# Late ZW rows in two column halves, the late rows of batches 4 to 7 behind later tiles, and three wide products beside the last weights

## The chip, the cores and the metric

The kernel runs on one core of a Trainium2 chip. TensorE (PE in the profile) multiplies matrices into PSUM banks of 128 partitions by 512 fp32 columns; PEld is its loading of stationary operands. VectorE is DVE, ScalarE is ACT, GpSimd is POOL, and SyncE (SP) only issues transfers here. The metric is the device time of one execution in microseconds, as the median of several runs.

## The reference

```python
# attention with a window of 128 and a bias that falls off with distance: 8 batches, 8 heads, 576 x 64
attn = softmax(where(mask, q @ k.T / 8 + bias, -1e9));  x = attn @ v      # heads joined: x is (8, 576, 512)
# mixing of modes
X  = rfft(x, axis=1)[:, :64]                   # 64 modes, complex
Yr = Xr @ w_r - Xi @ w_i;  Yi = Xr @ w_i + Xi @ w_r    # per mode a 512x512 matrix, two of them
y  = irfft(Y, n=576);  u = x + y
out = u + maximum(u @ w_ch, 0)
```

The two weight tensors w_r and w_i are 64 x 512 x 512 fp32 each, 134 MB in all; every byte is read once. The output is 9.44 MB of fp32.

## The kernel before

**Stages.** The attention runs over "units" (a pair of heads of one batch) while the first quarter of the weight rows streams in. Then the other three quarters of the weights stream in (from about 166 us on); TensorE multiplies each piece into an accumulator (`_modes`, L704) and between pieces prepares the end: `_xw` computes x + x @ w_ch per output tile and keeps it in two bf16 parts (`hl`), `_z_early` turns finished spectrum rows into Z (the spectrum itself) and ZW (the spectrum times w_ch) per batch.

**The tiles.** The output has 36 tiles of 128 rows by 512 columns (`g.seq`): four full tiles per batch, and after each odd batch one tile that holds the last 64 rows of two batches. Batch b of 0 to 7 comes in ascending order, so batches 4 to 7 begin at tile 18.

**The late rows.** The last modes are known only when the last weight piece has landed. Their spectrum rows (block 3 of `g.ZT`, 32 rows for each batch) are "late". `_modes` adds the last accumulator into ZT (DVE, L729). `_finish` then makes, for batches 0 to 3 and for batches 4 to 7, a late ZW (16 products of 128x512 in four column groups of TensorE, L790, tile `zlw`, cast to the bf16 tile `zl1`) and a late Z (16 products of 128x128, L794, tile `zlp`, cast to `zl0`). `_z_put` (POOL, L816) copies each batch's 32 late rows into the full Z or ZW tile.

**The end's loop.** For each tile, `g.u[i]` is a PSUM bank out of six. `_known(n)` starts it from `hl` (L745, a pair of products that share TensorE's columns); `_taken(n, 1)` adds the inverse transform of ZW (L825, a pair); `_greater(n)` takes the maximum with x on DVE (L845), which gives x + max(u @ w_ch, 0) and lacks only y; for the tiles in `RELU` it is a Relu on ACT (L843) and TensorE adds x by a further pair (L745). `_taken(i, 0)` adds y, the inverse transform of Z (a pair), ACT copies the bank to SBUF (L881, tile `o`, 16 buffers), and SP issues the transfer out (L886; the four tiles of two halves are two transfers, L889). The loop runs four tiles ahead (`AHEAD`): at tile i it starts tile i + 4. The first five tiles (`KNOWN`) are started before the last weights land and lack only their late rows; for them `_taken` uses the late tile directly. Each engine executes its instructions in the order in which the code emits them; there is no planner in this part.

In `_finish` the order was: late ZW of batches 0 to 3 (cast by ACT), late Z of 0 to 3 (cast by DVE), late ZW of 4 to 7 (cast by ACT), then the five known tiles' late products with the late Z of 4 to 7 after the second, then all 16 puts on POOL, then the loop.

**The last weight piece** arrives in three transfers (`LAST`: rows 0 to 2, 3 to 4, 5 of six), so the 24 products of the last `_modes` run as 12, 8 and 4, each group behind its own transfer.

Of the kernel before, what the change touches and what calls it, by code (L numbers as in the profile page):

```python
# [9 lines left out]
FP32 = mybir.dt.float32  # L10
BF16 = mybir.dt.bfloat16
# [5 lines left out]
P = 128  # L17
# [12 lines left out]
KNOWN = 5  # L30
# [2 lines left out]
FT_ROWS = (2, 3, 4, 5, 6)  # L33
FT_ORDERS = (10, 14, 18, 22)
WCH_ROWS = (1, 4)
RELU = (8, 16, 24, 32)
LAST = (0, 3, 5, 6)


# [5 lines left out]
def kernel(  # L45
# [52 lines left out]
    with tc.manual_schedule(engines={ET.SP, ET.PE, ET.Activation, ET.DVE, ET.Pool}):  # L98
        with ExitStack() as wctx:
# [129 lines left out]
            for m0, w in rest_w:  # L229
# [4 lines left out]
                if done in KNOWN_AT:  # L234
# [3 lines left out]
                    known = KNOWN_AT[done]  # L238
            mctx.close()
        _finish(g)  # L240


# [402 lines left out]
def _load_w(g):  # L645


    if g.loaded == len(g.parts):
        return False
    j, m0, w = g.parts[g.loaded]  # L650
    lo, hi = g.place[g.loaded]
    for u, z in g.place[g.used : g.loaded]:
        if u < hi and lo < z:
            return False
    g.loaded += 1
    r0 = GROUPS[j][0] * P
    src = (g.w_r, g.w_i)[w][m0 : m0 + JOINT[j], r0 : r0 + len(GROUPS[j]) * P]
    a = ROWS[j]
    cut = LAST if g.loaded == len(g.parts) else (0, a)
    for u, z in zip(cut, cut[1:]):  # L660
        g.nc.sync.dma_start(
            out=g.ring[:, lo + u * g.DM : lo + z * g.DM],
            in_=src.rearrange("m (p a) e -> p m (a e)", a=a)[:, :, u * g.DM : z * g.DM])
    return True
# [15 lines left out]
def _pair_of_modes(g, j, m0):  # L680
    for w in range(2):
        _modes(g, j, m0, w)
    if m0 % MB == MB // 2 - JOINT[j] and m0 + MB < g.NM:
        _select(g, j, m0 // MB * MB + MB)


def _modes(g, j, m0, w, last=False):


    nc = g.nc  # L690
    X = g.X[j, m0 // MB]
    assert g.parts[g.used] == (j, m0, w)
    lo, hi = g.place[g.used]
    wt = g.ring[:, lo:hi].bitcast(BF16)[:, 1::2].rearrange("p (a e) -> p a e", e=g.DM)
    ends = set(range(MB, g.NM + 1, MB)) | ({g.NM - 4, g.NM - 2} if last else set())
    if w == 0 and (m0 == 0 or m0 in ends):
        g.acc[j] = (m0, g.mpsum.tile([P, 4, 2, MB, 8], FP32, tag="acc", name="acc"))
    c0, acc = g.acc[j]
    R, n = ROWS[j], JOINT[j]
    order = [(et, a) for et in range(4) for a in range(R)]  # L700
    if g.used == len(g.parts) - 1:
        order = [(et, a) for u, z in zip(LAST, LAST[1:]) for et in range(4) for a in range(u, z)]
    for et, a in order:
        nc.tensor.matmul(  # L704
            acc[:, et, :, m0 - c0 : m0 - c0 + n, :],
            lhsT=wt[:, a, et * P : (et + 1) * P],
            rhs=X[:, a, 1 - w : 3 - w, m0 % MB : m0 % MB + n],
            start=(m0 == c0 and w == 0 and (et, a) == order[0]),
            stop=(m0 + n in ends and w == 1 and (et, a) == order[-1]))
    g.used += 1  # L710
    while _load_w(g):
        pass
    m = m0 + n - 1
    if w == 0 or m + 1 not in ends:
        return

    def rows(t):
        return t[:, c0 // 16, :, :, c0 % 16 : m % 16 + 1, :].rearrange("p e a m b -> p e a (m b)")

    acc = acc[:, :, :, 0 : m + 1 - c0].rearrange("p e a m b -> p e a (m b)")  # L720
    dst = rows(g.ZTa)
    if j == 0:
        nc.scalar.copy(dst, acc)
    else:
        o = dst
        if last:
            o = g.ZT[:, :, c0 // 16, :, c0 % 16 : m % 16 + 1, :].rearrange(
                "p e a m b -> p e a (m b)")
        nc.vector.tensor_tensor(out=o, in0=acc, in1=dst, op=ALU.add)  # L729


def _xt(g, n, pool, psum):
# [9 lines left out]
def _pair(nc, out, lhsT, rhs, **kw):  # L742

    for h in range(2):
        nc.tensor.matmul(  # L745
            out[64 * h : 64 * h + 64], lhsT=lhsT[h], rhs=rhs[h], tile_position=(0, 64 * h), **kw)


def _xw(g, n, xT, psum):
# [4 lines left out]
    xw = psum.tile([P, g.DM], FP32, tag="xw", bufs=2, name="xw")  # L754
    if n not in RELU:
        nc.tensor.matmul(xw, lhsT=g.ident_b, rhs=x, start=True, stop=False)
    for dt in range(4):
        nc.tensor.matmul(  # L758
            xw, lhsT=xT[:, dt], rhs=g.wch[:, dt],
            start=(dt == 0 and n in RELU), stop=(dt == 3))  # L760
    for h in range(2):
# [21 lines left out]
        nc.gpsimd.memset(g.ZW[b][32 * (b % 4) : 32 * (b % 4) + 32], 0.0)  # L783


def _z_product(g, ps, w, et, k, l):

    ks = slice(32 * k, 32 * k + 32)
    if w:
        g.nc.tensor.matmul(  # L790
            ps[ks], lhsT=l, rhs=g.wch[:, et], start=(et == 0), stop=(et == 3),
            tile_position=(0, 32 * k))
    else:
        g.nc.tensor.matmul(  # L794
            ps[ks, et], lhsT=l, rhs=g.ident_b, start=True, stop=True,
            tile_position=(0, 32 * k))


def _z_late(g, b0, w, pool, tag, copy):


    ps = g.eps.tile([P, 4, P], FP32, tag="zp", name="zlp") if w == 0 else (
        pool.tile([P, g.DM], FP32, tag=tag, name="zlw"))
    for et in range(4):
        for c in range(4):
            l = g.ZT[:, et, 3].rearrange("p a m b -> p (a m) b")[:, :, b0 + c]
            _z_product(g, ps, w, et, c, l)
    t = g.fin.tile([P, g.DM], BF16, tag=f"zl{w}", bufs=2, name=f"zl{w}")
    copy(t, ps if w else ps.rearrange("p a b -> p (a b)"))
    g.late[w, b0] = t  # L810


def _z_put(g, w, b):

    ks = slice(32 * (b % 4), 32 * (b % 4) + 32)
    g.nc.gpsimd.tensor_copy((g.Z, g.ZW)[w][b][ks], g.late[w, b // 4 * 4][ks])  # L816


def _taken(g, i, w, late=None):

    rows = slice(0, 32) if late else slice(0, P)
    for h, (b, s) in enumerate(g.seq[i][1]):
        o = slice(32 * (b % 4), 32 * (b % 4) + 32) if late else rows
        z = late if late else (g.Z, g.ZW)[w][b]
        g.nc.tensor.matmul(  # L825
            g.u[i][64 * h : 64 * h + 64], lhsT=g.FT[o, b % 4, s : s + 64], rhs=z[o],
            start=False, stop=(w == 0 or late is not None or i >= KNOWN),
            tile_position=(o.start, 64 * h), skip_group_check=(w == 0))


def _known(g, i):

    pool, tag = ((g.fps, "f0"), (g.fps, "f1"), (g.lps, "l0"), (g.lps, "l1"), (g.lps, "l2"),
                 (g.kps, "k0"))[i % 6]
    g.u[i] = pool.tile([P, g.DM], FP32, tag=tag, name="u")
    _pair(g.nc, g.u[i], [g.ident2] * 2, [g.hl[:, i, h] for h in range(2)],
          start=True, stop=False)


def _greater(g, i):  # L840

    if i in RELU:
        g.nc.scalar.activation(g.u[i], g.u[i], AF.Relu)  # L843
    else:
        g.nc.vector.tensor_tensor(out=g.u[i], in0=g.u[i], in1=g.seq[i][0], op=ALU.max)  # L845


def _finish(g):

    nc, tc = g.nc, g.tc
    N = len(g.seq)
    with ExitStack() as fctx:
        g.fin = pool = fctx.enter_context(tc.tile_pool(name="fin", bufs=16))
        g.kps = fctx.enter_context(
            tc.tile_pool(name="kps", bufs=1, space=bass.MemoryType.PSUM, side="right"))
        _z_late(g, 0, 1, g.eps, "zwp", nc.scalar.copy)
        _z_late(g, 0, 0, g.eps, "zp", nc.vector.tensor_copy)
        _z_late(g, 4, 1, g.kps, "k0", nc.scalar.copy)  # L860
        for i in range(KNOWN):
            _taken(g, i, 1, g.late[1, 0])
            _greater(g, i)
            if i == 1:
                _z_late(g, 4, 0, g.eps, "zp", nc.scalar.copy)
        for w, b in ((0, 0), (1, 1), (0, 1), (1, 0), (1, 2), (0, 2), (1, 3), (0, 3)):
            _z_put(g, w, b)
        for b in range(4, 8):
            for w in (1, 0):
                _z_put(g, w, b)  # L870
        for i in range(N):
            x, n = g.seq[i][0], i + AHEAD
            if i in RELU:
                _pair(nc, g.u[i], [g.ident_b[:, 0:64], g.ident_b[:, 64:128]], [x] * 2,
                      start=False, stop=True, skip_group_check=True)
            _taken(g, i, 0)
            if KNOWN <= n < N:
                _known(g, n)
                _taken(g, n, 1)
            o = pool.tile([P, g.DM], FP32, tag="o", name="o")  # L880
            nc.scalar.copy(o, g.u[i])  # L881
            if KNOWN <= n < N:
                _greater(g, n)
            _, (lo, hi) = g.seq[i]
            if hi == (lo[0], lo[1] + 64):
                nc.sync.dma_start(out=g.out[lo[0], lo[1] : lo[1] + P], in_=o)  # L886
            else:
                for h, (b, s) in enumerate((lo, hi)):
                    nc.sync.dma_start(out=g.out[b, s : s + 64], in_=o[64 * h : 64 * h + 64])  # L889
# [30 lines left out]
```

## Time and profile before

| what | value |
|---|---|
| runs before | 445.66, 448.30, 448.21 us; median 448.21 |
| the profiled execution | 450.29 us; the span of its instructions 448.5 us; mean granted clock 0.769 |
| busy | PE 294.1, PEld 204.2, DVE 216.1, ACT 189.6, POOL 139.1 us |
| DMA | 173.86 MB, mean 388 GB/s |
| stage from the last weight piece on (about 414 us) | 34 us |
| output transfers | 32 of 256 KB, 3.3 us median to landing; 8 of 128 KB, 3.1 us |

The page's second part cuts the span into 40 slices of 11.2 us; the digits give the busy tenths of each engine, the granted TensorE clock and the share of the DMA engines. Windows of the trace give the same for any stretch. The timeline gives groups of instructions in order of time, with the start, the duration, and in brackets the idle time of the engine before it and what ended that.

### The profile page before, as it was taken

What the parts mean: (1) busy time and instruction counts of PE and PEld (TensorE: products, weight loads), DVE (VectorE), ACT (ScalarE), POOL (GpSimd) and SP (SyncE); (2) the same over time, 40 slices, a digit from 0 to 9 for tenths busy, and PEclk for the clock granted to TensorE, in tenths of its full rate; (3) what the DMA queues carried; (4) which work ended last, traced back from release to release, by engine and by line L of the source; (5) the groups of instructions that cost most, each with busy time, mean ns of one, the idle gap of its engine ahead of it and who ended that gap; (6) DMA issues with size and microseconds to landing.
All of it is one profiled execution on the core that took longest, in us unless ns stands there. A gap on an engine that the chain in (4) does not pass through costs nothing.

```text
span 448.5 us, 12893 instructions
## 1 busy us (share of the span) xinstructions
PE 294.1 (66%) x5506; PEld 204.2 (46%) x5527; DVE 216.1 (48%) x427; ACT 189.6 (42%) x302; POOL 139.1 (31%) x257
## 2 busy tenths in 40 slices
PE   2467989887787885222235664854856748696993
PEld 2455767666666763111123333432433334464661
DVE  8458566566765661010002543453535345462882
ACT  3787656584866741000011331322313233251794
POOL 7699889586876702020000000000000000000700
PEclk9969576686988975555555988589778587899997
DMA  8999999999999999999999999999999999996498
GB/s 249 346 335 327 388 325 353 347 390 379 392 368 375 393 415 429 432 425 426 430 427 433 426 429 429 427 430 426 430 429 430 426 429 430 427 428 282 185 374 288
DMA packets 51562, 173.86 MB, mean 388 GB/s; under 512 B 4912, under 2 KB 21296, under 8 KB 43440
## 3 DMA queue, kind: packets, MB, share of 16 engines
q1 hardware_dynamic: 51120, 171.99, 97.2%
q0 software_dynamic: 384, 1.05, 0.9%
q8 instruction: 43, 0.70, 0.6%
q14 instruction: 15, 0.12, 0.1%
HBM read 163.58 MB, written 9.44 MB: 386 GB/s over the span
## 4 chain that ended last, share of the span: by engine, by line
DMA 50%; PE 26%; ACT 10%; DVE 6%; issue 4%; POOL 2%; ACTq 0%; POOLq 0%
DMA ring<-in_moe_w_r_dram 47%; ACT att L459 6%; PE acc L704 5%; PE sc L447 4%; PE xt L539 4%; PE u L825 3%; PE av L493 3%; DMA ring<-in_moe_w_i_dram 3%; ACT qkT L428 3%; PE tqk L420 2%; PE u L745 2%; POOL qkb L397 1%; PE xw L758 1%; DVE x_sb L507 1%; ACT mask L311 1%
## 5 line engine op out<-in xcount | busy, mean ns | idle before, releaser
L704 PE MATMUL acc<-Xz,ring 128*128 128x32 bf16 x2048 | 70.7, 183 | 100.2 <-DMA ring<-in_moe_w_r_dram 51.0
L704 PEld LDWEIGHTS <-ring 128*128 128x128 bf16 x2048 | 61.3, 101 | 130.1 <-DMA ring<-in_moe_w_r_dram 65.1
L763 ACT CAST hl<-xw 64x512 bf16<-64x512 f32 x72 | 41.7, 579 | 105.6 <-PE xw L758 70.9
L459 ACT ACTIVATE att<-sc 128x1024 bf16<-128x1024 f32 x64 | 65.6, 1025 | 32.8 <-PE sc L447 26.7
L764 DVE TENSOR_TENSOR hl<-xw,hl 64x512 bf16<-64x512 f32 x72 | 49.6, 688 | 58.1 <-ACT hl L763 57.8
L409 POOL CAST vb<-v 64x256 bf16<-64x256 f32 x128 | 64.7, 505 | 20.1 <-PE av L493 13.7
L783 POOL MEMSET ZTa<- 32x512 bf16 x2 | 1.0, 515 | 187.5 <-ACT ZTa L781 187.5
L447 PE MATMUL sc<-qkT,qkT 64*64 64x256 bf16 (+1 forms) x512 | 32.4, 330 | 30.1 <-ACT qkT L428 16.3
L758 PE MATMUL xw<-wch,xT 128*128 128x512 bf16 x138 | 46.3, 467 | 2.7 <-issue 2.2
L428 ACT COPY qkT<-tqk 128x576 bf16<-128x576 bf16 x64 | 40.7, 638 | 0.6 <-PE tqk L420 0.6
L420 PE MATMUL tqk<-ident_b,qkb 64*64 64x64 bf16 x1152 | 31.7, 214 | 7.6 <-POOL qkb L397 6.9
L420 PEld LDWEIGHTS <-qkb 64*64 64x64 bf16 x1152 | 30.8, 130 | 10.2 <-POOL qkb L397 9.2
L464 DVE TENSOR_TENSOR att<-att,mask 128x1024 bf16<-128x1024 bf16 x32 | 26.9, 839 | 14.7 <-ACT att L459 14.5
L585 ACT ACTIVATE Xz<-xz 128x192 bf16<-128x192 f32 (+1 forms) x24 | 7.5, 313 | 59.0 <-DVE Xz L584 57.9
L493 PE MATMUL av<-vb,att 128*128 128x65 bf16 (+1 forms) x512 | 30.8, 215 | 0.6 <-issue 0.2
L584 DVE CAST Xz<-xz 128x384 bf16<-128x384 f32 (+1 forms) x24 | 12.0, 511 | 36.4 <-PE xz L578 35.7
L447 PEld LDWEIGHTS <-qkT 64*64 64x64 bf16 x512 | 13.1, 120 | 35.3 <-ACT qkT L428 18.8
L397 POOL CAST qkb<-k 128x576 bf16<-128x576 f32 x32 | 27.5, 859 | 0.0
L493 PEld LDWEIGHTS <-att 128*128 128x128 bf16 (+1 forms) x512 | 24.4, 111 | 6.5 <-issue 0.6
L397 POOL CAST qkb<-q 128x576 bf16<-128x576 f32 x32 | 24.6, 768 | 6.1 <-PE tqk L420 3.3
L738 DVE COPY xT<-tp 128x512 bf16<-128x512 bf16 x36 | 15.2, 421 | 21.9 <-PE tp L736 21.4
L469 DVE TENSOR_TENSOR att<-att,mask 128x1024 bf16<-128x1024 bf16 x32 | 25.0, 780 | 1.5 <-ACT att L459 1.1
(104 smaller groups left out, 395.2 us busy)
## 6 DMA issues: line engine op xcount, KB each, us to landing
ring<-in_moe_w_r_dram SPq DMA_DIRECT2D x32, 1536.0 KB, 13.8
ring<-in_moe_w_i_dram SPq DMA_DIRECT2D x31, 1536.0 KB, 13.7
ring<-in_moe_w_i_dram SPq DMA_DIRECT2D x33, 512.0 KB, 8.0
ring<-in_moe_w_r_dram SPq DMA_DIRECT2D x32, 512.0 KB, 7.4
q<-in_q_dram SPq DMA_DIRECT2D x32, 288.0 KB, 6.3
k<-in_k_dram SPq DMA_DIRECT2D x32, 288.0 KB, 6.2
v<-in_v_dram SPq DMA_DIRECT2D x64, 128.0 KB, 5.8
out_dram<-o SPq DMA_DIRECT2D x32, 256.0 KB, 3.3
```

What stands on the lines that cost most here:

```text
L397: g.nc.gpsimd.tensor_copy(tb, t)
L409: g.nc.gpsimd.tensor_copy(o[64 * r : 64 * r + 64, i], v[64 * i : 64 * i + 64, r])
L420: g.nc.tensor.transpose(tp[hs, r, :], u.b[w][hs, r], g.ident_b[hs, hs], tile_position=(64 * hh, 64 * hh))
L428: g.nc.scalar.copy(dst.rearrange("c (p r) -> c p r", r=g.R), u.tp[w].rearrange("c r p -> c p r"))
L447: nc.tensor.matmul(sc[64 * r : 64 * r + 64, hh, 256 * i : 256 * i + nq], lhsT=kT[hs, c * P + r : c * P + P : 2], rhs=qT[hs, c * P : c * P ...
L459: nc.scalar.activation(a, sc, AF.Exp, scale=1.0 / math.sqrt(g.D))
L464: nc.vector.tensor_tensor(out=a, in0=a, in1=m, op=ALU.mult)
L493: nc.tensor.matmul(av[o, hh, col(t)], lhsT=att[c // 2][:, hh, q0 : q0 + m], rhs=u.vb[:, 2 * c + hh, 0 : D + 1], start=(j == 0), stop=(t < ...
L704: nc.tensor.matmul(acc[:, et, :, m0 - c0 : m0 - c0 + n, :], lhsT=wt[:, a, et * P : (et + 1) * P], rhs=X[:, a, 1 - w : 3 - w, m0 % MB : m0 ...
L758: nc.tensor.matmul(xw, lhsT=xT[:, dt], rhs=g.wch[:, dt], start=(dt == 0 and n in RELU), stop=(dt == 3))
L763: nc.scalar.copy(g.hl[own, n, h], xw[own])
L764: nc.vector.tensor_tensor(out=g.hl[other, n, h], in0=xw[own], in1=g.hl[own, n, h], op=ALU.subtract)
```

## The change

The diff touches `_finish` and what it calls, one set of tile numbers, and the last `_modes`.

- `RELU` becomes (8, 13, 15, 24, 32) in place of (8, 16, 24, 32): tiles 13 and 15 take the Relu on ACT and the added pair on TensorE, tile 16 takes the maximum on DVE. `_xw` accordingly leaves out the product with the identity for 13 and 15 and makes it for 16.
- Around the last weight piece, `_wide` makes one 128x512 product of the identity with w_ch into the bank `zp`, whose result is not used: before the second group, before the third, and after the last.
- The late ZW of batches 0 to 3 is made in two column halves, in the banks `zwp` and `k0`: 16 products of 256 columns, cast by ACT; 16 products of 256 columns, cast by DVE. The late Z of 0 to 3 is cast by ACT. For tile 0, the late product is made once per half.
- The late ZW of batches 4 to 7 moves into the loop: four of its 16 products behind each of tiles 3, 5, 7 and 9, the cast on DVE and one put on POOL behind tile 9. The late Z of 4 to 7 follows behind tile 11, with its cast on DVE and the other seven puts.

```diff
-RELU = (8, 16, 24, 32)
+RELU = (8, 13, 15, 24, 32)
+ZW_LATE = (3, 5, 7, 9)
+Z_LATE = 11
...
     for et, a in order:
+        if g.used == len(g.parts) - 1 and (et, a) in [(0, u) for u in LAST[1:-1]]:
+            _wide(g)
         nc.tensor.matmul(
...
+    if g.used == len(g.parts) - 1:
+        _wide(g)
     g.used += 1
...
+def _wide(g):
+
+    ps = g.eps.tile([P, 4, P], FP32, tag="zp", name="wide")
+    g.nc.tensor.matmul(
+        ps.rearrange("p a b -> p (a b)"), lhsT=g.ident_b, rhs=g.wch[:, 0], start=True, stop=True)
...
-        _z_late(g, 0, 1, g.eps, "zwp", nc.scalar.copy)
-        _z_late(g, 0, 0, g.eps, "zp", nc.vector.tensor_copy)
-        _z_late(g, 4, 1, g.kps, "k0", nc.scalar.copy)
+        sides = [slice(0, g.DM // 2), slice(g.DM // 2, g.DM)]
+        zl = _late(g, 0, 1)
+        for c, p, tag, copy in (
+                (sides[0], g.eps, "zwp", nc.scalar.copy),
+                (sides[1], g.kps, "k0", nc.vector.tensor_copy)):
+            ps = p.tile([P, g.DM], FP32, tag=tag, name="zlw")[:, c]
+            _z_late(g, 0, 1, range(4), ps, c)
+            copy(zl[:, c], ps)
+        zp = g.eps.tile([P, 4, P], FP32, tag="zp", name="zlp")
+        _z_late(g, 0, 0, range(4), zp)
+        nc.scalar.copy(_late(g, 0, 0), zp.rearrange("p a b -> p (a b)"))
         for i in range(KNOWN):
-            _taken(g, i, 1, g.late[1, 0])
+            for c in sides if i == 0 else [slice(0, g.DM)]:
+                _taken(g, i, 1, zl, c, last=(c.stop == g.DM))
             _greater(g, i)
-            if i == 1:
-                _z_late(g, 4, 0, g.eps, "zp", nc.scalar.copy)
...
-        for b in range(4, 8):
-            for w in (1, 0):
-                _z_put(g, w, b)
         for i in range(N):
...
+            if i in ZW_LATE:
+                if i == ZW_LATE[0]:
+                    zwp = g.eps.tile([P, g.DM], FP32, tag="zwp", name="zlw")
+                _z_late(g, 4, 1, [ZW_LATE.index(i)], zwp)
+            if i == ZW_LATE[-1]:
+                nc.vector.tensor_copy(_late(g, 4, 1), zwp)
+                _z_put(g, 1, 4)
+            if i == Z_LATE:
+                zp = g.eps.tile([P, 4, P], FP32, tag="zp", name="zlp")
+                _z_late(g, 4, 0, range(4), zp)
+                nc.vector.tensor_copy(_late(g, 4, 0), zp.rearrange("p a b -> p (a b)"))
+                for w, b in ((0, 4), (1, 5), (0, 5), (1, 6), (0, 6), (1, 7), (0, 7)):
+                    _z_put(g, w, b)
             o = pool.tile([P, g.DM], FP32, tag="o", name="o")
```

More of the change, by code (lines that the diff above doesn't have):

```diff
@@ L783, in _z_early, with _z_product @@
         nc.gpsimd.memset(g.ZW[b][32 * (b % 4) : 32 * (b % 4) + 32], 0.0)
-def _z_product(g, ps, w, et, k, l):
+def _z_product(g, ps, w, et, k, l, cols=slice(0, 512)):
     ks = slice(32 * k, 32 * k + 32)
@@ L790, in _z_product @@
         g.nc.tensor.matmul(
-            ps[ks], lhsT=l, rhs=g.wch[:, et], start=(et == 0), stop=(et == 3),
+            ps[ks], lhsT=l, rhs=g.wch[:, et, cols], start=(et == 0), stop=(et == 3),
             tile_position=(0, 32 * k))
@@ L796, in _z_product, with _z_late, _late @@
             tile_position=(0, 32 * k))
[L799 to L804, printed above, removed]
+def _z_late(g, b0, w, ets, ps, cols=slice(0, 512)):
+    for et in ets:
         for c in range(4):
             l = g.ZT[:, et, 3].rearrange("p a m b -> p (a m) b")[:, :, b0 + c]
[L807 to L810, printed above, removed]
+            _z_product(g, ps, w, et, c, l, cols)
+def _late(g, b0, w):
+    g.late[w, b0] = g.fin.tile([P, g.DM], BF16, tag=f"zl{w}", bufs=2, name=f"zl{w}")
+    return g.late[w, b0]
 def _z_put(g, w, b):
@@ L816, in _z_put, with _taken @@
     g.nc.gpsimd.tensor_copy((g.Z, g.ZW)[w][b][ks], g.late[w, b // 4 * 4][ks])
-def _taken(g, i, w, late=None):
+def _taken(g, i, w, late=None, cols=slice(0, 512), last=True):
     rows = slice(0, 32) if late else slice(0, P)
@@ L825, in _taken @@
         g.nc.tensor.matmul(
-            g.u[i][64 * h : 64 * h + 64], lhsT=g.FT[o, b % 4, s : s + 64], rhs=z[o],
-            start=False, stop=(w == 0 or late is not None or i >= KNOWN),
+            g.u[i][64 * h : 64 * h + 64, cols], lhsT=g.FT[o, b % 4, s : s + 64],
+            rhs=z[o, cols],
+            start=False, stop=last and (w == 0 or late is not None or i >= KNOWN),
             tile_position=(o.start, 64 * h), skip_group_check=(w == 0))
```

## The prediction

> **What bounds the kernel now.** I read the slices of the page first, then windows of the end, then its timeline, and last the landing times of the transfers out.
>
> ```profile
> PE   2467989887787885222235664854856748696993
> PEclk9969576686988975555555988589778587899997
> DMA  8999999999999999999999999999999999996498
> 412.38:415.79 3.41, 2.32 (x48) 1.46 (x47) 0.29 (x1) 0.00 (x0) 0.00 (x0) 1.00 0.12 48
> 415.79:419.20 3.41, 3.41 (x68) 1.73 (x62) 2.45 (x4) 2.01 (x4) 2.09 (x4) 1.00 0.01 2
> 429.44:439.68 10.24, 10.24 (x98) 6.73 (x96) 8.73 (x14) 9.53 (x18) 0.00 (x0) 1.00 1.01 370
> 439.68:443.10 3.42, 1.29 (x11) 0.50 (x6) 0.83 (x2) 2.29 (x5) 0.00 (x0) 1.00 1.00 359
> ```
>
> The DMA engines are full in nearly every slice; the hole is the 37th and 38th (403.6 to 426.1 us). The clock (tenths) changes while weights stream and is high in the last slices. Until about 412 us the weights set the time and nothing of the change lies on their path. In the windows (length; busy PE, PEld, DVE, ACT, POOL; clock; DMA share; GB/s) the DMA engines stand nearly still from 412.4 to 419.2 and are then full to the end. So the end has two parts: about 5 us from the last weights to the first transfer out, and some 27 us in which 9.44 MB go out. In the second part PE is busy without a gap as well.
>
> ```profile
> 414.51 0.29 DVE L729 TENSOR_TENSOR ZT<-acc,ZTa 128x128 bf16<-128x128 f32 x1 [5.90 <-PE acc L704]
> 414.86 1.09 PE L790 MATMUL zlw<-wch,ZT 128*32 128x512 bf16 x16 [0.38 <-DVE ZT L729]
> 416.00 0.58 ACT L809 CAST zl<-zlw 128x512 bf16<-128x512 f32 x1 [6.63 <-PE zlw L790]
> 416.01 1.05 PE L790 MATMUL zlw<-wch,ZT 128*32 128x512 bf16 x16
> 417.00 0.62 PE L825 MATMUL u<-zl,FT 32*64 32x512 bf16 x4
> 417.44 6.88 DVE L845 TENSOR_TENSOR u<-u,x_sb 128x512 f32<-128x512 f32 x11 [0.51 <-PE u L825]
> 417.54 0.47 PE L794 MATMUL zlp<-ident_b,ZT 128*32 128x128 bf16 x16
> 418.50 0.70 PE L825 MATMUL u<-ZTa,FT 128*64 128x512 bf16 x4
> 418.94 2.82 ACT L881 COPY o<-u 128x512 f32<-128x512 f32 x5 [0.29 <-PE u L825]
> 419.55 4.74 SPq L886 DMA_DIRECT2D out_dram<-o  x8
> 442.27 2.02 SPq L886 DMA_DIRECT2D out_dram<-o  x4
> ```
>
> This is the first part as a chain: ZT, late ZW, cast, tile 0's late product, its maximum, its last product, its copy, its transfer. Between 416.01 and 418.0 PE also does the late rows of batches 4 to 7, which no tile before 18 needs. The last line is the tail: the last four issues; the copy they wait for had ended at 442.27, the last issue began at 443.89 and landed at 447.30.
>
> **The first part, changed.** Late ZW: 16 products of 512 columns take 0.92 us (414.86 to the next group at 415.78). With 256 columns the streaming halves, but there are 16 weight loads in each half, and 16 such loads of the late Z take 0.41 (417.54 to 417.95) to 0.49 us. I take 0.49 a half (bounds 0.46, half of 0.92, and 0.66, PEld's own busy time for 16): the two halves end at 415.84 instead of 415.78, no gain by themselves. The gain is in what follows. The second half's cast on DVE starts at about 416.05 and costs 0.42 (128x256 from PSUM, L584, 421 ns) in place of ACT's 0.585; ACT's half (between 330 ns for 192 columns, L585, and 585 for 512; by a straight line 0.38) is over before. Late Z takes 0.41, to 416.25. Tile 0's second half goes at about 416.55 instead of 417.00, since the second late ZW (416.01 to 416.93) is no longer ahead of it. Its maximum runs from 416.9 to 417.6. The other four known tiles need 4 x 0.2155 = 0.86 (a pair every 0.2155 us, from 422.24, 422.46, 422.68, 422.89), to 417.5. Late Z of 0 to 3 is now cast by ACT behind its half: 416.5 to 417.1; the first put on POOL (0.60) ends at 417.75. So tile 0's last product goes at about 417.8 instead of 418.49: **0.7 us earlier**, and the first transfer at 418.9. Bounds: 0.35 if the halves are bound by loads at 0.66 each, 0.85 if they take 0.46 and ACT's cast is not late.
>
> **The loop, changed.** PE does 3 pairs a tile, 0.645 us, and never waits; what is added there comes out later, tile by tile. Late ZW of 4 to 7: four products behind each of four tiles, 0.92 / 4 = 0.23 each (bounds 0.2155, one stream of 512 columns, and 0.27), 0.92 in all. Late Z: 0.41 (0.23 to 0.47). RELU has one tile more: one pair, 0.2155. Sum 1.55 us (1.3 to 1.8). Against 0.7 gained at the start, PE is earlier by 0.7 up to tile 3, level at about tile 9, and **0.85 us later from tile 17 to the end**. DVE gains two casts of 0.69 and loses one maximum of 0.70, and at tiles 9 and 11 the casts stand where the maxima of 13 and 15 stood; behind them wait the maxima of 14 and 16, which PE needs 3 us later. ACT gains a Relu of 0.58 in the loop (ahead of it, its three casts become one and a half); it is busy 9.53 of 10.24, so two Relus within three tiles press it, for about 0.5 us, under a lead of four tiles. Puts: 0.61 each; the first of batch 4 ends near 426.6, tile 18's first use is at tile 14, near 428.7; the seven others run from 427.8 to 432, and the next user is tile 18 at 431.2, which needs only the first two. With late casts this cover of 2 us goes, and each us beyond is a stop of PE. SP's list is the same.
>
> **Wide products.** 0.2155 each, in PE's gaps of 0.45 (413.14 to 413.59, waiting for the second transfer), 0.25 (to 414.21) and 0.38 (to 414.86, waiting for DVE's ZT). They cost nothing there; if the three transfers land together, the first two cost 0.43. The loss of two identity products in `_xw` and the gain of one (0.2 us each) lie under PE's 51 us of waiting for weights.
>
> The row on the clock: the window 412.38 to 415.79 has PE at 68% and the clock stays at 1.00; windows of 3.41 us at 26 to 32% (340.70, 364.59) were each followed by 0.50. [...]
>
> **The transfers out.** A tile's 128 rows go at 0.636 us a tile (landings 437.12, 437.75, 438.38 ...), 22.9 us for 36. First bytes moved at 420.43, last near 446.6: 26.2 us, so 3.3 us were lost. Two losses stand out: blocks of code for PE (queue q8, 16 KB a packet) at 420.30 for 1.33 us and 434.62 for 0.94 us; around the second no tile landed between 434.68 and 437.12, 1.8 us more than the rhythm. [...] Both loads stay: the first shifts by about 24 PE instructions, to near 421.2, the second some 40 instructions earlier, to near 433.
>
> Sum: the stream can start at 419.7, 0.7 earlier, and would end 0.7 earlier if it never waited. But from tile 12 on PE's lead is gone: tile 18 is ready for the stream (issue plus 0.87 to the first byte) at about 433.5, when the stream is through tile 17 at 432.9; it waits 0.5. In the tail, PE's 0.85 is hidden: SP's last issues lag the copies by 1.6 us, and the last landing comes 3.41 us after its issue where 2.6 is the shortest. Result: -0.7 + 0.5 = **-0.2 us**. On the profiled execution 450.29 - 0.2 = 450.1; that execution is 2.1 over the median, and I take the difference onto the median: **448.0 us**.
>
> **Rivals.**
> - *The early start is passed on whole* (stream never waits, because the first code load leaves a queue of finished tiles): -0.7, 447.5. For it: transfers were full from 422.5. Against it: issues and copies kept step up to tile 18 (2.65 us to landing, the shortest).
> - *PE's debt decides, slower*: the loop becomes PE's from tile 9 on, copies and SP keep no lag, and the last landing follows PE's end by as much as before: +0.85, 449.1. It decides if the lag of 1.6 us at SP's tail was made of its own issue time (0.5 to 0.65 an issue) and is made again behind later copies. For it: SP's last seven issues are spaced by SP alone. Against it: that lag grew behind one issue of 1.14 us at 434.92, during the code load.
> [...]
> - *The change misses its aim*: halves bound by loads, start only 0.35 earlier, debt 1.2: about +0.3, 448.5.
>
> **How the numbers follow.** Forecast 0.42, passed on whole 0.18, PE's debt 0.18, clock 0.10, aim missed 0.12. Cases run from 446.5 to 449.1; the bounds of the unknown costs add 0.4 on either side, and the three runs of before lie 2.6 apart, so a median moves by about 1: 445.5 to 449.8. About 1% (4.5 us) is what a measurement of this kernel can tell from no change, and no case comes near it: faster 0.03, same 0.94, slower 0.03.
>
> **What would show it.** First transfer issued near 418.9 after ZT at the same time; four groups of 0.23 us of `zlw` in the loop; PE's last product near 441.7 instead of 440.9; DMA below full for half a us around 433. I am wrong if PE stops in the loop (puts or casts late), if the three weight transfers bunch, or if the clock falls to 0.50 in the end.

## The result

The changed kernel is **slower by 0.44%**: the ratio to the kernel before is 1.0044 with a 95% interval of 1.0024 to 1.0064; medians 449.83 us (22 runs, 447.31 to 453.66) against 448.03 us (22 runs, 445.52 to 451.23). On 448 us that is 2.0 us, with an interval of 1.1 to 2.9 (the medians alone differ by 1.8). The forecast was 0.2 us faster; the measured median lies 0.03 us above the upper end of the range, on the side of the rival "PE's debt decides".

### The profile page after: what moved, and what is told of

Same layout as the page of the kernel before. It is cut to its first block, busy times and chain, and to the rows that moved or that the text cites. A ratio compares the mean times of both kernels' runs of the same rounds, so it can differ in the third digit from the quotient of the medians.

```text
span 446.8 us, 12938 instructions
## 1 busy us (share of the span) xinstructions
PE 296.9 (66%) x5528; PEld 202.8 (45%) x5549; DVE 217.0 (49%) x428; ACT 190.2 (43%) x302; POOL 138.3 (31%) x257
## 3 DMA queue, kind: packets, MB, share of 16 engines
q0 software_dynamic: 384, 1.05, 1.0%
## 4 chain that ended last, share of the span: by engine, by line
DMA 60%; PE 23%; ACT 7%; DVE 4%; issue 3%; SPq 2%; POOL 1%; ACTq 0%; POOLq 0%
DMA ring<-in_moe_w_r_dram 46%; DMA ring<-in_moe_w_i_dram 7%; PE acc L708 4%; DMA v<-in_v_dram 4%; ACT att L461 4%; DMA k<-in_k_dram 3%; PE u L838 3%; PE xt L541 3%; PE sc L449 3%; PE av L495 2%; ACT qkT L430 2%; PE u L758 2%; PE tqk L422 2%; SPq L364 1%; PE xw L771 1%
## 5 line engine op out<-in xcount | busy, mean ns | idle before, releaser
L708 PE MATMUL acc<-Xz,ring 128*128 128x32 bf16 x2048 | 69.8, 183 | 99.5 <-DMA ring<-in_moe_w_i_dram 50.8
L708 PEld LDWEIGHTS <-ring 128*128 128x128 bf16 x2048 | 60.4, 101 | 129.6 <-DMA ring<-in_moe_w_i_dram 63.6
L411 POOL CAST vb<-v 64x256 bf16<-64x256 f32 x128 | 61.2, 478 | 23.1 <-PE av L495 16.2
L771 PE MATMUL xw<-wch,xT 128*128 128x512 bf16 x139 | 45.2, 456 | 2.6 <-issue 2.0
L422 PE MATMUL tqk<-ident_b,qkb 64*64 64x64 bf16 x1152 | 32.6, 217 | 9.1 <-POOL qkb L399 8.6
L495 PE MATMUL av<-vb,att 128*128 128x65 bf16 (+1 forms) x512 | 32.2, 220 | 0.5 <-DVE att L471 0.3
L495 PEld LDWEIGHTS <-att 128*128 128x128 bf16 (+1 forms) x512 | 25.6, 115 | 6.7 <-issue 0.9
L399 POOL CAST qkb<-q 128x576 bf16<-128x576 f32 x32 | 26.5, 829 | 4.4 <-PE tqk L422 1.6
```

The source lines that it names most:

```text
L399: g.nc.gpsimd.tensor_copy(tb, t)
L411: g.nc.gpsimd.tensor_copy(o[64 * r : 64 * r + 64, i], v[64 * i : 64 * i + 64, r])
L422: g.nc.tensor.transpose(tp[hs, r, :], u.b[w][hs, r], g.ident_b[hs, hs], tile_position=(64 * hh, 64 * hh))
L495: nc.tensor.matmul(av[o, hh, col(t)], lhsT=att[c // 2][:, hh, q0 : q0 + m], rhs=u.vb[:, 2 * c + hh, 0 : D + 1], start=(j == 0), stop=(t < ...
L708: nc.tensor.matmul(acc[:, et, :, m0 - c0 : m0 - c0 + n, :], lhsT=wt[:, a, et * P : (et + 1) * P], rhs=X[:, a, 1 - w : 3 - w, m0 % MB : m0 ...
L771: nc.tensor.matmul(xw, lhsT=xT[:, dt], rhs=g.wch[:, dt], start=(dt == 0 and n in RELU), stop=(dt == 3))
```

## The profile after

The span of the profiled execution is 446.8 us, shorter than the 448.5 us before, although the kernel is slower. The two executions differ in when the last weights arrive, which the change does not touch: DVE finished ZT at 414.81 us before and at 411.63 us after. So everything below is counted from the end of that ZT. The slices and, for the end, four windows of the changed kernel (columns as before: length; busy PE, PEld, DVE, ACT, POOL; clock; DMA share; GB/s):

```profile
PE   2578889887887885232236565665766549688993
PEclk9999856686698885555556996868879888899998
DMA  8999999999999999999999999999999999995598
411.34:415.46 4.12, 3.57 (x69) 2.16 (x69) 2.53 (x6) 1.57 (x4) 1.67 (x3) 1.00 0.01 2
415.46:429.44 13.98, 13.98 (x142) 6.76 (x140) 11.23 (x18) 11.24 (x20) 7.21 (x14) 1.00 0.79 290
429.44:439.68 10.24, 10.24 (x96) 5.45 (x92) 8.66 (x14) 9.27 (x19) 0.55 (x1) 1.00 0.97 347
439.68:443.10 3.42, 0.21 (x2) 0.00 (x0) 0.00 (x0) 1.51 (x4) 0.00 (x0) 0.99 0.99 345
```

The hole before the first transfer is 4.12 us from the start of ZT's addition, where it was 5.04 (414.51 to 419.55). But in the 14 us that follow, PE is busy without a gap and the DMA engines run at a share of 0.79, where it was 0.92 in the same 13.98 us behind the first issue before (419.55 to 433.53): they wait for tiles. The timeline of the changed kernel shows both:

```profile
411.34 0.29 DVE L735 TENSOR_TENSOR ZT<-acc,ZTa 128x128 bf16<-128x128 f32 x1 [6.21 <-PE acc L708]
411.68 1.10 PE L803 MATMUL zlw<-wch,ZT 128*32 128x256 bf16 x32 [0.16 <-DVE ZT L735]
412.83 0.42 DVE L879 CAST zl<-zlw 128x256 bf16<-128x256 f32 x1 [1.21 <-PE zlw L803]
413.64 4.88 DVE L859 TENSOR_TENSOR u<-u,x_sb 128x512 f32<-128x512 f32 x8 [0.39 <-PE u L838]
414.40 0.41 PE L838 MATMUL u<-ZTa,FT 128*64 128x512 bf16 x2
415.00 0.41 PE L838 MATMUL u<-ZTa,FT 128*64 128x512 bf16 x2 [0.19 <-DVE u L859]
415.46 3.37 SPq L917 DMA_DIRECT2D out_dram<-o  x5
416.72 0.41 PE L838 MATMUL u<-ZTa,FT 128*64 128x512 bf16 x2
417.06 0.44 PE L803 MATMUL zlw<-wch,ZT 128*32 128x512 bf16 x4
417.43 0.41 PE L838 MATMUL u<-ZTa,FT 128*64 128x512 bf16 x2
417.67 0.38 PE L758 MATMUL u<-hl,ident 128*64 128x512 bf16 x2
424.12 0.38 PE L838 MATMUL u<-ZTa,FT 128*64 128x512 bf16 x2
424.43 0.47 PE L807 MATMUL zlp<-ident_b,ZT 128*32 128x128 bf16 x16
424.83 0.41 PE L838 MATMUL u<-ZTa,FT 128*64 128x512 bf16 x2
439.14 2.05 ACT L912 COPY o<-u 128x512 f32<-128x512 f32 x4 [0.29 <-PE u L838]
```

Lines 8 to 10 are the first moved group of four late products between two pairs. Pair, group and pair begin at 416.72, 417.06 and 417.43: 0.71 us from pair to pair, of which a pair takes 0.2155, and the pair behind the group is followed after 0.24 instead of 0.2155. This group cost 0.52 us, not the 0.23 forecast. The next three cost 0.49 each, and the late Z (lines 12 to 14) 0.52 us: 2.5 us for the five, **0.50 us on average**. Yet each of the four ZW groups streams 512 columns like any pair (four products side by side; 16 in one stretch took 0.92 us before). DVE is not what delays them: the trace puts the weight load behind the first group down to DVE's maximum, but behind the next three, as dear to 0.03 us, it names no other engine. The last line ends at 441.19, 29.56 us after ZT; before, the last copy ended at 442.27, 27.46 us after ZT.

| us after the end of ZT | before | after |
|---|---|---|
| tile 0's last product | 3.69 | 2.77 |
| first transfer issued | 4.75 | 3.83 |
| last copy by ACT ends | 27.46 | 29.56 |
| last transfer issued | 29.08 | 30.75 |
| last transfer landed | 32.49 | 33.96 |

The start gained 0.92 us; the loop from tile 0's last product to the last copy grew from 23.77 to 26.79 us, by 3.0; the copies are 2.1 us late at the end, and the last landing 1.5.

## The experiments

Three theories, and a fourth that was added later. **A**: PE pays for each change of the column width (pairs of 64, late products of 32 columns), and its lateness moves the end. **B**: the moved work costs only what it streams; the casts and Relus on DVE and ACT around tiles 9 to 15 delay the loop. **C**: the wide products, or the transfers out. **D** (the later one): the loads of PE's code set the end.

The ratios below are to the kernel before. dose32, dose64, dose128 and nohalf were executed once, under the profiler, so their traces are read and not their times; every figure "after ZT" is from one profiled execution.

### cols64: the moved products in two groups of 64 columns

```diff
+def _z_late64(g, b0, w, ets, ps):
...
+        for h in range(2):
+            l = g.ZL[:, et, 64 * h : 64 * h + 64]
+            hs = slice(64 * h, 64 * h + 64)
+            if w:
+                g.nc.tensor.matmul(
+                    ps[hs], lhsT=l, rhs=g.wch[:, et], start=(et == 0), stop=(et == 3),
+                    tile_position=(0, 64 * h))
...
+        g.ZL = pool.tile([P, 4, P], BF16, tag="ZL", bufs=1, name="ZL")
+        nc.scalar.copy(
+            g.ZL.rearrange("p e (b r) -> p e b r", b=4),
+            g.ZT[:, :, 3].rearrange("p e a m b -> p e b (a m)")[:, :, 4:8])
...
-                _z_late(g, 4, 1, [ZW_LATE.index(i)], zwp)
+                _z_late64(g, 4, 1, [ZW_LATE.index(i)], zwp)
...
-                _z_late(g, 4, 0, range(4), zp)
+                _z_late64(g, 4, 0, range(4), zp)
```

> The changed kernel, but the late products of batches 4 to 7 in the loop are made from a batch-major copy of their ZT rows (one more ACT copy, right after ZT) in two groups of 64 columns instead of four of 32: the same streaming, the same column width as the pairs around them. Theory A (switching the column width between the 64-column pairs and the 32-column late products costs PE about 0.29 us for each of the five groups, since its weight loads are not made ahead across the switch): a group costs 0.22 us instead of 0.50 to 0.52, from ZT's end to the end of the last copy 28.0 us instead of 29.6, to the last landing about 32.8 instead of 34.0, ratio to the kernel before 0.999 to 1.001. Theory B (the moved products cost what they stream, and the loss comes from the casts and Relus on DVE and ACT around tiles 9 to 15): a group costs 0.5 us still, 29.5 us to the last copy, ratio 1.004. Theory C (the wide products or the transfers out): no change either, 1.004.

Ratio 1.0001 (0.9979 to 1.0024). The last copy ended 28.18 us after ZT, the last landing came at 32.57. PE's timeline of this kernel, around the same group:

```profile
416.24 0.41 PE L854 MATMUL u<-ZTa,FT 128*64 128x512 bf16 x2
416.46 0.41 PE L827 MATMUL zlw<-wch,ZL 128*64 128x512 bf16 x2
416.67 0.41 PE L854 MATMUL u<-ZTa,FT 128*64 128x512 bf16 x2
416.89 0.41 PE L758 MATMUL u<-hl,ident 128*64 128x512 bf16 x2
```

Every start is 0.2155 behind the one before, and all five groups cost 0.22 us. With the same streaming, the same casts, Relus, puts and wide products, the loop lost 1.4 of its 3.0 us of growth. B and C as the main cause fall. The edit changes three things at once, though: the column width, the number of products in a group (half as many), and the layout that the weights are read from; the doses below take them apart.

### oneblock: all of it in one stretch behind tile 9

```diff
-ZW_LATE = (3, 5, 7, 9)
-Z_LATE = 11
+ZW_LATE = (9,)
+Z_LATE = 9
...
-                _z_late(g, 4, 1, [ZW_LATE.index(i)], zwp)
+                _z_late(g, 4, 1, range(4), zwp)
```

> The changed kernel with all late products of batches 4 to 7 behind tile 9 in one stretch (16 of ZW, then 16 of Z, 32 columns each). Theory A: one switch there and back instead of five: 0.92 + 0.41 + 0.29 = 1.6 us instead of 2.6 in the loop, the last copy ends 28.5 us after ZT instead of 29.6, ratio about 1.002. Theory B: the casts follow each other even more closely, 29.6 or later, ratio 1.004 or more. Theory C: 29.6, 1.004.

Last copy 28.45, last landing 33.54, ratio 1.0009 (0.9989 to 1.0029). The stretch cost 1.41 us where the five groups cost 2.5: five excursions made into one take 1.1 us off the loop with not one product less, as A has it. The landing gained only 0.4 (33.54 for 33.96), and the times cannot tell this kernel from the one before, nor clearly from the changed one.

### nowide: without the three wide products

```diff
-        if g.used == len(g.parts) - 1 and (et, a) in [(0, u) for u in LAST[1:-1]]:
-            _wide(g)
...
-    if g.used == len(g.parts) - 1:
-        _wide(g)
```

> The changed kernel without the three wide products (their result is used by nobody). Theory A: nothing on the path, ZT to the last copy 29.6 us, ratio 1.004, granted clock 1.00 through the end. Theory C (the wide products stand in the way of the last weights' products or of the late ZW): the late ZW starts earlier after the last product of the weights by up to 0.2 us, ratio 1.000 to 1.003. If the wide products keep the clock up: it falls to 0.50 at the start of the end in some executions, and the ratio is above 1.005.

Ratio 1.0043 (1.0016 to 1.007), last copy 29.57, the start to the hundredth as in the changed kernel (first transfer at 3.83). The granted clock is 1.00 from ZT to the last copy in this profile too. So the wide products cost nothing, and no effect on the clock is seen in the times.

### relu_before: RELU as before

```diff
-RELU = (8, 13, 15, 24, 32)
+RELU = (8, 16, 24, 32)
```

> The changed kernel with RELU as before (8, 16, 24, 32): one pair less on PE, one Relu less on ACT, DVE does the maxima of 13 and 15 besides its two casts. Theory A: one pair, 0.22 us less on PE: last copy 29.3 us after ZT, ratio 1.0035 to 1.004. Theory B: the copies between tiles 9 and 16 come 0.5 us or more earlier or later than in the changed kernel, as ACT or DVE decides them: last copy 28.8 if the Relus were the loss, 30.2 if DVE now stops PE.

Last copy 29.35, 0.21 earlier: one pair on PE. Ratio 1.0031 (1.001 to 1.0052). Neither Relus nor maxima hold the loop up. The last landing came at 34.22, 0.26 later than in the changed kernel although the copies were earlier; the section on the prediction comes back to this.

### dose32, dose64, dose128: the price by itself

All three are the kernel before, with one unused group of products behind each of the eight tiles 3, 5, ... 17. This is dose32; dose64 has two products of 64 columns in place of the four of 32, dose128 one of 128.

```diff
+def _dose(g):
+
+    ps = g.eps.tile([P, g.DM], FP32, tag="zwp", name="dose")
+    for c in range(4):
+        g.nc.tensor.matmul(
+            ps[32 * c : 32 * c + 32], lhsT=g.ident_b[:, 32 * c : 32 * c + 32], rhs=g.wch[:, 0],
+            start=True, stop=True, tile_position=(0, 32 * c))
...
+            if i in (3, 5, 7, 9, 11, 13, 15, 17):
+                _dose(g)
```

> The kernel before, with four products of 128x512 on 32 columns each (result unused, into the free bank zwp) behind each of the eight tiles 3, 5, ... 17: the disputed cost alone, without any move of work, cast or Relu. Theory A (switch of column width): each group costs 0.50 us on PE, so tile 0's last product to the end of the last copy takes 23.7 + 4.0 = 27.7 us. Theory B (what is streamed): 8 x 0.22, 25.5 us.

> The same eight places, but one pair of products of 128x512 on 64 columns each: the same streaming time as dose32 in the column width of the pairs around it. Theory A: 8 x 0.22, so 25.5 us from tile 0's last product to the end of the last copy, 2.2 us less than dose32. Theory B: as dose32.

> The kernel before with one product of 128x512 on all 128 columns (result unused) behind each of the tiles 3, 5, ... 17: the same streaming as dose32 and dose64. If any change of the column width costs (64 to 128 as well as 64 to 32): 0.40 to 0.45 us a group, the last copy 3.2 to 3.6 us later than before, at 30.7 to 31.1 after ZT. If only narrow groups do: 0.22 a group, 29.2.

PE's timeline around one group, dose32 first, then dose64, then dose128:

```profile
418.30 0.41 PE L825 MATMUL u<-ZTa,FT 128*64 128x512 bf16 x2
418.64 0.40 PE L852 MATMUL dose<-wch,ident_b 128*32 128x512 bf16 x4
418.97 0.41 PE L825 MATMUL u<-ZTa,FT 128*64 128x512 bf16 x2
419.21 0.38 PE L745 MATMUL u<-hl,ident 128*64 128x512 bf16 x2
```

```profile
419.48 0.41 PE L825 MATMUL u<-ZTa,FT 128*64 128x512 bf16 x2
419.69 0.41 PE L852 MATMUL dose<-wch,ident_b 128*64 128x512 bf16 x2
419.91 0.41 PE L825 MATMUL u<-ZTa,FT 128*64 128x512 bf16 x2
420.12 0.41 PE L745 MATMUL u<-hl,ident 128*64 128x512 bf16 x2
```

```profile
420.90 0.38 PE L825 MATMUL u<-ZTa,FT 128*64 128x512 bf16 x2
421.21 0.39 PE L851 MATMUL dose<-wch,ident_b 128*128 128x512 bf16 x1
421.53 0.41 PE L825 MATMUL u<-ZTa,FT 128*64 128x512 bf16 x2
421.77 0.38 PE L745 MATMUL u<-hl,ident 128*64 128x512 bf16 x2
```

| kernel | last copy ends after ZT | a group | last landing after ZT |
|---|---|---|---|
| before | 27.46 | - | 32.49 |
| dose64 | 29.18 | 1.72 / 8 = 0.215 | 33.35 |
| dose32 | 31.06 | 3.60 / 8 = 0.45 | 35.22 |
| dose128 | 31.01 | 3.55 / 8 = 0.44 | 35.18 |

The same 512 columns cost 0.215 us in the width of their neighbours and 0.44 to 0.45 in a wider or a narrower one: 0.23 us for an excursion, about half of it on each side of the group (in dose32 the starts into and out of the group lie 0.34 and 0.33 us apart, in dose128 0.31 and 0.32, in dose64 0.21 and 0.22). It is the change of width that costs, not narrowness, and not the number of products (four or one). The moved products of the changed kernel cost 0.50, 0.05 more, with weights that they read from ZT at a stride where these read the identity; that this is the reason was not tried apart. And in all three the landing is late by 0.86 to 0.87 us less than the last copy: in these three profiles the tail behind the copies covers that much. So A stands for what PE pays; how much of its lateness reaches the last landing is taken up further below.

### nohalf: without the column halves

```diff
-        for c, p, tag, copy in (
-                (sides[0], g.eps, "zwp", nc.scalar.copy),
-                (sides[1], g.kps, "k0", nc.vector.tensor_copy)):
-            ps = p.tile([P, g.DM], FP32, tag=tag, name="zlw")[:, c]
-            _z_late(g, 0, 1, range(4), ps, c)
-            copy(zl[:, c], ps)
+        ps = g.eps.tile([P, g.DM], FP32, tag="zwp", name="zlw")
+        _z_late(g, 0, 1, range(4), ps)
+        nc.scalar.copy(zl, ps)
...
-        nc.scalar.copy(_late(g, 0, 0), zp.rearrange("p a b -> p (a b)"))
+        nc.vector.tensor_copy(_late(g, 0, 0), zp.rearrange("p a b -> p (a b)"))
...
-            for c in sides if i == 0 else [slice(0, g.DM)]:
+            for c in [slice(0, g.DM)]:
```

> The changed kernel without the column halves: the late ZW of batches 0 to 3 in one bank of 512 columns, cast whole by ACT, late Z cast by DVE as before. If the halves bring half of the earlier start: the first transfer is issued 4.1 to 4.2 us after ZT's end, against 3.83 in the changed kernel and 4.75 before. If the moved rows of batches 4 to 7 bring all of it: 3.8.

The first transfer was issued 4.09 us after ZT. Of the 0.92 us gained at the start, 0.66 come from the rows of batches 4 to 7 being out of the way and 0.26 from the halves together with what goes with them (the casts shared out anew and tile 0's late product in two). The loop behind it took as long as in the changed kernel (last copy 26.79 us after tile 0's last product, in both).

### pad_before: the code load moved ahead

```diff
+                    if done == 44:
+                        ps = g.eps.tile([P, g.DM], FP32, tag="zp", name="pad")
+                        for _ in range(32):
+                            nc.tensor.matmul(
+                                ps[:, 0:1], lhsT=g.ident_b, rhs=g.ident_b[:, 0:1],
+                                start=True, stop=True)
```

> The kernel before with 32 products of one column (64 PE instructions, result unused) in an idle stretch of PE at the 44th weight piece, which moves PE's code loads some 64 instructions earlier in the work. Theory D (a block of code that is loaded during the transfers out stops one DMA engine, and the end with it, for 1.3 to 2 us): the load that stood 5.5 us after ZT comes at about 3 us, before the first transfer's bytes, the first landing comes 2.1 instead of 3.4 us after its issue, and the ratio is 0.996 to 0.998. If the loads are hidden: 1.000.

The code loads came at 2.74 and 16.12 us after ZT instead of 5.49 and 19.81, and the first landing 2.07 us after its issue instead of 3.37: the load does hold up the transfers beside it. But the last landing came at 32.55 (before 32.49), ratio 1.0002 (0.9973 to 1.0031). The 1.3 us that tile 0 gained were gone by tile 13, which landed at 16.47 (before 16.38); tiles 0 to 13 landed 2.1 to 3.1 us after their issue, so the stream had caught up with them. Then the second load came, and no tile landed from 16.47 to 18.90, as none had from 19.87 to 22.31 before. So D falls for the first load. The second was moved and not taken away, and D stays open for it.

### best and bestpad: what the findings point to

`best` is cols64 with RELU as before and the four ZW groups behind tiles 0, 1, 5 and 9; `bestpad` adds the 32 idle products of pad_before.

```diff
-RELU = (8, 13, 15, 24, 32)
-ZW_LATE = (3, 5, 7, 9)
+RELU = (8, 16, 24, 32)
+ZW_LATE = (0, 1, 5, 9)
```

> cols64 with RELU as before (8, 16, 24, 32) and the four late ZW groups behind tiles 0, 1, 5 and 9 instead of 3, 5, 7 and 9: in cols64 PE stands still for 0.38 us between the last products of tiles 0 and 1, waiting for DVE's maximum, so the first group should cost nothing. Theory A with PE's debt as what moves the end: the last copy ends 27.7 to 27.8 us after ZT (cols64 28.18, before 27.46), the last landing at 32.0 to 32.5 (cols64 32.57, before 32.49), ratio 0.998 to 1.000. If the transfers out alone set this end: 32.5 again.

> best with the 64 idle PE instructions of pad_before at the 44th weight piece, so that the first code load of the end comes before the first transfer's bytes. If the code loads, not PE, limit the end once PE's debt is gone: the last landing 31.2 to 31.8 us after ZT, ratio 0.996 to 0.999. If PE's last copy limits it still: as best.

`best`: last copy 27.72, last landing 32.38, ratio 0.9995 (0.9971 to 1.0019). `bestpad`: 27.71 and 32.17, ratio 0.9993 (0.9972 to 1.0015). The copies came as expected, the last landing of `bestpad` did not reach the 31.2 to 31.8 of its first case, and a code load still lay among its transfers at 15.92. The traces show 0.1 and 0.3 us gained against the kernel before, which the times cannot tell from nothing. Neither is shown to beat it. PE's added work in the loop uses up the whole early start (0.92) and 0.26 us more, by which the last copy of `best` is later than before.

## Why the prediction was wrong

**The start: right, mis-sized.** Forecast 0.7 us earlier (0.35 to 0.85), measured 0.92. The two halves took 0.93 us (411.68 to 412.61; forecast 0.98) and the moved rows out of the way brought most of it, as worked out. What was mis-sized is the wait for the late Z: its cast by ACT was forecast 1.69 us after ZT and began at 1.45, so that the first put, forecast to end last, ended with tile 0's maximum at 2.7.

**The loop: the step that failed.** "Late ZW of 4 to 7: four products behind each of four tiles, 0.92 / 4 = 0.23 each (bounds 0.2155, one stream of 512 columns, and 0.27)" and "Late Z: 0.41 (0.23 to 0.47)". The five groups cost 0.49 to 0.52 each. The 0.92 was read from 16 products in one unbroken stretch of one width; four of them between pairs of another width pay the change twice. The upper bound of 0.27 had no row behind it that contained a change. Such a row was there: the late Z ahead of the known tiles' products, begun at 417.54 although the pair before it would have let it begin at 417.43, and 0.41 us long where its streaming (16 products of 128 columns, four side by side, 512 columns in all) is an estimated 0.2155 at the rate of the pairs. Two rows of the kernel before, beside those that the prediction shows, make the pair:

```profile
415.78 0.41 PE L794 MATMUL zlp<-ident_b,ZT 128*32 128x128 bf16 x16
417.95 0.62 PE L825 MATMUL u<-zl,FT 32*64 32x512 bf16 x6
```

The late Z at 415.78, between products of its own width, was followed after 0.23 us (at 416.01); the one at 417.54, between products of another, after 0.41 (at 417.95). The prediction read the 0.41 as the time of 16 weight loads. The runs show that such a change costs time, 0.23 us for there and back in dose32 and dose128 and 0.28 in the changed kernel. In the trace of the changed kernel the weight load of the first moved group begins together with its products, at 417.06, where the load of the pair before it began 0.22 us ahead of that pair (416.50 for 416.72). The prediction weighed no such cost.

The growth of 3.0 us is made up of 5 x 0.50 = 2.5, one pair of 0.22 for the Relu tile, and 0.30 at the first tiles, which the forecast also lacked: tile 0 goes out earlier, but the next maxima on DVE follow at 0.6 us each, and PE waits (eight maxima in 4.88 us from 413.64, and the 0.19 in brackets at 415.00; the copies of tiles 1 to 3 follow tile 0's after 0.59, 1.28 and 1.88 us instead of 0.48, 0.98 and 1.58). 3.0 less the 0.92 of the start is the 2.1 us by which the last copy is late; the forecast had 0.85.

**The tail: right in some profiles, not a fixed amount.** The forecast hid a debt of 0.85 us behind SP's issues and the landings. What is hidden is how late the last copy is, less how late the last landing is, both against the kernel before. That is 0.86 us in dose64 (1.72 on the copies, 0.86 on the landing) and 0.88 in nowide, but 0.63 of the 2.1 in the changed kernel, 0.64 in cols64, 0.16 in relu_before and nothing in oneblock (copies 0.99 late, landing 1.05). So a few tenths in the last landing of one profile prove nothing, and what sets the hidden amount was not tried apart.

**The transfers out: the place of the wait was wrong, the part of the loads stays open.** The forecast had the stream of transfers wait 0.5 us (its own figures, 433.5 and 432.9, give 0.6) and only at tile 18. In the trace it waited earlier and longer: the shares of 0.79 and 0.92 over 13.98 us differ by an estimated 1.8 us, and tiles 12 to 15 landed 2.0 to 2.3 us after their issue, where the shortest before was 2.65. The first code load was forecast at 6.4 us after ZT and came at 6.35, the second at 18.2 against 19.24. That such loads hold up transfers is shown: pad_before moved both, and both delays moved with them. Whether the 1.8 us of the second count into the end, as the prediction has it, is not settled. In all thirteen profiles a code load lies among the transfers and no tile lands for 1.9 to 2.7 us beside it. In the kernel before, the 16 tiles behind that pause then landed every 0.64 us on average to the very end, which speaks for the prediction. In the changed kernel the pause began with 16 tiles landed instead of 19. This may be how PE's lateness reaches the end; no run takes the load away.

**The rivals.** "PE's debt decides, slower" (0.18) is what came, with 1.5 us in the trace and 2.0 in the times for its 0.85, since the debt was 2.1. Its condition, that SP's lag of 1.6 us behind the copies is made again, held in part: the lag was 1.2. The 0.10 for the clock, whose case is the 446.5 at the lower end, stood for an end that begins at half clock. No run shows this term: the granted clock was 1.00 from ZT to the last copy in the profiles of both kernels and in nowide, and the times without the wide products showed no difference (1.0043 for 1.0044). The wide products cost nothing, as forecast, and in the loop PE waited for no put and no cast; the identity products in `_xw` were not tried apart.

**What can be told apart.** The prediction took about 1% as the least that the runs can tell from no change. With 22 runs of each kernel 0.44% stood clear of it.

## What to carry to other kernels

When work is moved between other work on TensorE, price it from a row where it stands between the same neighbours, not from a dense stretch of its own kind; here a change of the column width and back cost 0.23 us, as much again as a product of 512 columns. Where the moved products could take their neighbours' width, that cost was gone (cols64, 0.22 us a group); in one block it was paid once (oneblock, 1.41 us in place of 2.5). A hole filled at the start was worth nothing by itself here, since PE had no gap afterwards: it gave 0.92 us, and the same products then cost 2.5 us in the loop.

## What had not been expected

- A product of 512 columns cost 0.215 us among its own width and 0.44 to 0.45 us between others, for 32 and for 128 columns alike.
- Code loads moved by 64 idle PE instructions brought the first landing forward by 1.3 us and the last one by nothing; the pause of the landings beside the second load moved with it, by 3.4 us.
- The execution with the shorter span was that of the slower kernel: the time at which the last weights arrive differed by 3.2 us between the two profiles, more than the whole effect, so only times counted from a common event could be compared.
